# Gating the first eight raw weight loads of a fused attention and mixer kernel on the softmax broadcasts, in the plan that orders its instructions

## The chip, the cores and the metric

The kernel runs on one core of a Trainium2 chip. The metric is device time in microseconds (us) of one execution; of several runs the median counts. One further execution was taken with the hardware profiler; all rows below come from that one. PE is TensorE, with PEld for its weight loads; DVE is VectorE, ACT ScalarE, POOL GpSimd. SP, ACT and POOL issue the transfers between memories.

## The reference

Attention over 4 batches and 12 heads feeds a token mixer of rank 32 and a channel mixer. Cut to what matters:

```python
scores = cap * np.tanh((scale * q @ k.T) / cap)      # 448 x 448 a head, head_dim 64
attn = np.exp(scores - max); attn /= attn.sum(-1)
x = (attn @ v) laid out as [4, 448, 768]
h = x.transpose(0, 2, 1) @ U @ V                     # rank 32 over the tokens
u = x + h.transpose(0, 2, 1)
out = u + np.maximum(u @ w_ch1, 0.0) @ w_ch2         # 768 -> 3072 -> 768
```

## The kernel before

All work is written as tasks with estimated durations, buffers and priorities. `Plan.simulate` plays them through a list scheduler at build time: each engine takes the ready task of the lowest priority number. `emit` then writes the instructions in the order found. On the chip every engine and every issuing queue runs its own list in that order, and waits only where a semaphore for a real tile says so. A key in a task's `r` or `w` that is no tile (such as `("rd", p)`) orders tasks in the plan alone.

The first stage is attention, in groups of four of the 24 head pairs (`four`). A pair's scores are made on PE (`sc`, line 493), go through tanh (498) and exp (508) on ACT into `th`, are summed on DVE into `es` (540), and are multiplied with the values on PE (534) into `u`. For every second pair, p = 1, 3, ..., 23, `normalize(p)` runs what is called a chain here: sums over tokens on PE (573), a copy `sr`, a transfer `r<-sr` (580), a reciprocal on DVE (589), a transfer `rd<-r` to memory (584), and two transfers `rb<-rd` (597) that broadcast the rows over 64 partitions each. DVE multiplies `u` by `rb` (602, the norm), and only then can PE transpose `u` for the token mixer (`mixin`, 624). The three transfers are issued by POOL. There are 12 chains, the n-th for p = 2n - 1.

The second stage, the channel mixer, runs on PE from its first product (851) to the end, 12 steps of two row blocks of `w_ch1` and of `w_ch2` each, for two batches at a time. The weights come as 64-bit words. `block` loads a raw block of 768 KB into `wr` (SP queue, 720), ACT and DVE convert it into `wa` (`convert`: ACT 335, DVE 340 and 343, here called the join), ACT stores the result as `kept` (724), and DVE and ACT split it into parts (`ta` and `ws`, lines 691, 286 and 698). `wr` has two buffers, `wa` two during attention; blocks 1 to 4 serve the first step of the second stage, block 5 and on the next. One more `wr` buffer, between blocks 4 and 5, holds sums of `u`.

SP's queue issues `qk` (467) and `vn` (473), the inputs of attention, and the raw blocks, in one order. In what follows w1 to w5 are the loads of blocks 1 to 5.

Of the kernel before, what the change touches and what calls it, by code (L numbers as in the profile page):

```python
# [64 lines left out]
    ("operands", 56),  # L65
)
SLOW = {"four.load": 1.24, "normalize.spread": 1.00, "normalize.put": 1.25, "normalize.get": 0.72, "block.load": 1.02, "four.tanh": 1.99}
FILL, FIRST = 18, 5


# [220 lines left out]
class Build(Plan):  # L291
# [266 lines left out]
    def normalize(self, p):  # L558

        nc = self.nc  # L560
        prio = p - 100
        e = self.es[p - 1], self.es[p]
        rth, rj = self.rest[p]
        rest = p >= SUMS
        s = self.psum("misc")
        sr = self.buf("sr", [128, S], F32, self.an)
        r7 = self.buf("r7", [128, S // 32], F32, self.aq)
        u = self.u_bufs[p // NP]
        dram = {}

        def sums():
            for i in range(4):
                nc.tensor.matmul(
                    s.t[32 * i:32 * i + 32, :S], self.ones[:, 0], e[i % 2].t[:, i // 2], start=True, stop=not rest)
            for i in range(4 if rest else 0):
                nc.tensor.matmul(
                    s.t[32 * i:32 * i + 32, :S], self.ones[:, 1 + i % 2], rth.t[:, rj, i // 2], start=False, stop=True)

        def spread():
            nc.gpsimd.dma_start(out=r7.t, in_=sr.t[::32].rearrange("h (p f) -> h p f", p=32))  # L580

        def put():
            d = dram[0] = self.dp.tile([4, S], F32, tag="rd", name="rd", bufs=4)
            nc.gpsimd.dma_start(out=d.rearrange("a (p f) -> (a p) f", p=32), in_=r7.t)

        self.task({"PE": 1500 if rest else 750}, sums, r=[(e[0], 0), (e[1], 0), *([(rth, rj)] if rest else [])], w=[(s, 0)], prio=prio, mode="s")
        self.task({"DVE": 620, "ACT": 560}, lambda e: self.copy(e, sr.t, s.t[:, :S]), r=[(s, 0)], w=[(sr, 0)], prio=prio)
        self.task({"POOL": 700}, spread, r=[(sr, 0)], w=[(r7, 0)], lat=3000, prio=prio)
        self.task({"DVE": 250}, lambda: nc.vector.reciprocal(r7.t, r7.t), w=[(r7, 0)], prio=prio)
        self.task({"POOL": 600}, put, r=[(r7, 0)], w=[("rd", p)], lat=2500, prio=prio)  # L590
        rb = self.buf("rb", [128, 2, S], F32, self.an)
        q = p % NP - 1

        def get():
            rows = dram[0].rearrange("(a i) s -> a (i s)", a=2)
            for a in range(2):
                nc.gpsimd.dma_start(
                    out=rb.t[64 * a:64 * a + 64].rearrange("p i s -> p (i s)"), in_=rows[a:a + 1].broadcast_to((64, 2 * S)))

        def norm():  # L600
            x = u.t[:, q:q + 2]
            nc.vector.tensor_tensor(out=x, in0=x, in1=rb.t, op=ALU.mult)

        self.task({"POOL": 1100}, get, r=[("rd", p)], w=[(rb, 0)], lat=3400, prio=prio)
        self.task({"DVE": 1090}, norm, r=[(rb, 0)], w=[(u, q), (u, q + 1)], prio=prio, lock=True)

    def mixin(self, b, pp):
# [101 lines left out]
    def block(self, which, f, first, begin, prio):  # L709

        nc = self.nc
        a = self.buf("wa", [128, DM], F32, self.wp, self.late)
        if not first:
            self.task({"SP": 350}, lambda: nc.sync.dma_start(out=a.t, in_=self.kept[which, f]),
                r=[("kept", which, f)], w=[(a, 0)], lat=4000, prio=prio)
            return a
        raw = self.buf("wr", [128, 2 * DM], I32, self.wq)

        def load():
            nc.sync.dma_start(out=raw.t, in_=self.w[which][f].bitcast(I32))  # L720

        def keep():
            d = self.kept[which, f] = self.dp.tile([128, DM], F32, tag="kept", name="kept", bufs=2 * NF)
            nc.scalar.dma_start(out=d, in_=a.t)

        self.task({"SP": 350}, load, w=[(raw, "u"), (raw, "l")], lat=7500, prio=prio, begin=begin)
        self.convert(raw, lambda: raw.t, a, lambda: a.t, prio, DM)
        self.task({"ACT": 120}, keep, r=[(a, 0)], w=[("kept", which, f)], lat=6500, prio=prio)
        return a
# [37 lines left out]
    def moe(self):  # L767


        self.kept = {}  # L770
        order, pend = 10, None
        for n, bs in enumerate(((0, 1), (2, 3))):
            made = {}
            if not n:
                made[0] = self.prepare(0, True, 20000, ALONE - 90)
            xs = self.operands(bs, ORDER if n else EARLY, -50 if n else ALONE - 90)
            vs = self.buf("vs", [128, 3, S], F32, self.g1) if n else None
            gq, last, down, turns = {}, None, iter(()), [2] * 7
            for c in range(NCH):
                fs = [c * CF + i for i in range(CF)]  # L780
                ws, w1 = made.get(c) or self.prepare(c, n == 0, 0, 3 if n or c < NCH - 2 else -60)
                gs = {}
                if pend:
                    down, turns = self.down(order, *pend), [2] * 7
                    pend = None
                elif gq and c % 2 == 0:
                    down = self.down_seven(order, bs, c // 2 - 1, gq, vs)
                    gq = {}
                if n:
                    turns = [2] * 7 if not c else [1 + (i + c) % 2 for i in range(7)]  # L790
                if n and c == 0:
                    for _ in down:
                        pass
                    order += 12
                if n and c % 2 == 0:
                    pools = (self.g0, self.gw, self.g1) if c % 4 else (self.gw, self.g1, self.g0)
                    last = {(b, j): self.buf("gq", [128, 2, S], F32, *pools) for b, j in ((1, 1), (0, 0), (0, 1), (1, 0))}
                for k, _ in zip(turns, self.up_seven(bs, fs, xs, ws, gs, order, last if n else None, c % 2)):
                    for _ in range(k):
                        next(down, None)  # L800
                if not n or c % 2 or c == 0:
                    for _ in down:
                        pass
                if n:
                    if c % 2:
                        gq = last
                else:
                    pend = bs, fs, w1, gs
                order += 20
        self.last_sums(bs, vs)  # L810
        for _ in self.down_seven(order + 10, bs, PAIRS - 1, gq, vs):
            pass
# [209 lines left out]
    def down_seven(self, order, bs, m, gq, vs):  # L1022
# [4 lines left out]
        u0, u1 = (self.u_bufs[b] for b in bs)  # L1027
        block = lambda u, d: ((lambda: u.t[:, d]), (u, d))
        onto = {3: lambda d: block(u1, d), 1: lambda d: block(u0, d), 6: lambda d: block(u0, 3 + d), 5: lambda d: block(vs, d),
            2: lambda d: block(u0, d), 7: lambda d: block(u1, 3 + d), 4: lambda d: block(u0, 3 + d)}  # L1030
        if final:
            at = range(order, order + 21)
# [61 lines left out]
    def rank(self):  # L1094

        for t in self.tasks:
# [7 lines left out]
            if t.lat:  # L1104
                t.lat *= next((k for x, k in SLOW.items() if stage.startswith(x)), 1)

# [56 lines left out]
```

## Time and profile before

| | us |
|---|---|
| median of 3 runs | 853.18 |
| the runs | 852.47 to 858.34 |
| the profiled execution | 853.6 |
| its span, first to last instruction | 851.8 |
| busy in the span: PE / DVE / ACT / POOL | 840.4 / 691.0 / 527.6 / 146.1 |

The span is what the trace shows; the profiled execution is 1.8 us longer by the device's own clock, and 0.4 us above the median of the runs. Busy time of PE counts overlapping matmuls once, and a matmul's end is modelled.

### The profile page before, as it was taken

Reading aid. Unit: us, or ns where it says so; the run is one execution under the profiler, and the core shown is the slowest. Engines: PE = TensorE matmul, PEld = TensorE weight load, DVE = VectorE, ACT = ScalarE, POOL = GpSimd, SP = SyncE. Lnnn points to the kernel's source line nnn. Section 1 sums busy time; section 2 is a strip of 40 time slices with the busy share of each in tenths; the row PEclk is TensorE's granted clock in tenths of the full one; section 3 lists DMA queues with packets and bytes.
Section 4 is the critical chain, followed back from the end, with each engine's and each line's share of the span. In section 5 each row is a group of like instructions: output and inputs, shape, how many; then the busy total and the mean of one; then the engine's idle time right before and its main releaser. Section 6 shows DMA issues by size and latency. Waiting matters only on the chain. (4 is left out here: it accounts for less than half of the span.)

```text
span 851.8 us, 11737 instructions
## 1 busy us (share of the span) xinstructions
PE 840.4 (99%) x4264; PEld 671.4 (79%) x4264; DVE 691.0 (81%) x1144; ACT 527.6 (62%) x789; POOL 146.1 (17%) x188
## 2 busy tenths in 40 slices
PE   9999999998999999999999999999999999999998
PEld 5334334346899999999999899999999999999997
DVE  2799889999887777877778699789888788888786
ACT  7999899885555355545555465456655555656472
POOL 0111111111022122122122122102111111111142
PEclk9999999999999999999999999999999999999999
DMA  6752443423578878787877866714427354262479
GB/s 225 241 172 84 160 148 96 146 68 93 183 190 259 245 188 249 191 265 211 231 231 207 252 162 151 215 48 120 114 36 179 68 143 93 53 170 42 122 136 224
DMA packets 51354, 136.51 MB, mean 160 GB/s; under 512 B 6720, under 2 KB 27104, under 8 KB 51296
## 3 DMA queue, kind: packets, MB, share of 16 engines
q1 hardware_dynamic: 23024, 79.29, 28.3%
q0 software_dynamic: 21360, 37.59, 24.6%
q10 hardware_dynamic: 6912, 18.88, 5.7%
q8 instruction: 33, 0.54, 0.3%
q14 instruction: 25, 0.20, 0.1%
HBM read 79.28 MB, written 24.47 MB: 122 GB/s over the span
## 5 line engine op out<-in xcount | busy, mean ns | idle before, releaser
L851 PE MATMUL mm<-x,ws 128*128 128x448 f32 x1512 | 332.7, 367 | 1.4 <-ACT cx L284 0.8
L851 PEld LDWEIGHTS mm<-x,ws 128*128 128x128 f32 x1512 | 283.3, 188 | 27.3 <-ACT cx L284 1.2
L916 PE MATMUL mm<-g,w 128*128 128x448 f32 x864 | 187.0, 366 | 0.6 <-DVE cx L864 0.3
L916 PEld LDWEIGHTS mm<-g,w 128*128 128x128 f32 x864 | 162.0, 188 | 15.0 <-ACT st L284 0.9
L1049 PE MATMUL mm<-g,w 128*128 128x448 f32 x696 | 154.9, 366 | 0.0
L284 ACT ACTIVATE st<-mm 128x448 f32<-128x448 f32 x133 | 72.4, 544 | 113.7 <-PE mm L916 55.2
L1049 PEld LDWEIGHTS mm<-g,w 128*128 128x128 f32 x696 | 130.6, 188 | 11.8
L929 POOL DMA_DIRECT2D u<-st x72 | 62.5, 868 | 268.9 <-ACT st L284 263.8
L1084 POOL DMA_DIRECT2D u<-st x57 | 49.4, 866 | 224.1 <-ACT st L284 161.4
L498 ACT ACTIVATE th<-sc,qsc 128x896 f32<-128x896 f32 x84 | 80.3, 1005 | 11.9 <-PE sc L493 11.7
L493 PE MATMUL sc<-qk 64*128 64x448 f32 (+1 forms) x384 | 77.8, 573 | 0.0
L508 ACT ACTIVATE th<-th,capt 128x1792 f32<-128x1792 f32 x42 | 75.2, 1790 | 0.8
L921 DVE TENSOR_TENSOR u<-u,mm 128x448 f32<-128x448 f32 x72 | 44.5, 618 | 21.6 <-PE mm L916 19.9
L534 PE MATMUL o<-th,vn 128*64 128x448 f32 x288 | 59.4, 548 | 0.0
L493 PEld LDWEIGHTS sc<-qk 64*128 64x128 f32 (+1 forms) x384 | 27.2, 175 | 37.2 <-issue 18.9
L343 DVE SCALAR_TENSOR_TENSOR wa<-wa,wr 128x768 int32<-128x768 int32 (+2 forms) x50 | 46.7, 935 | 11.1 <-ACT wa L335 10.3
L698 DVE TENSOR_TENSOR ws<-ta,ws 128x384 fp32r<-128x384 f32 x96 | 53.0, 552 | 3.2 <-ACT ws L284 2.9
L1079 DVE TENSOR_TENSOR u<-u,mm 128x448 f32<-128x448 f32 x57 | 35.0, 619 | 23.3 <-PE mm L1049 21.7
L540 DVE TENSOR_TENSOR es<-es,th 128x896 f32<-128x896 f32 (+1 forms) x44 | 47.5, 1082 | 6.0 <-ACT th L508 5.5
L335 ACT ACTIVATE wa<-wr 128x768 f32<-128x768 f32 (+2 forms) x50 | 44.1, 884 | 3.8 <-DVE wr L340 2.4
L534 PEld LDWEIGHTS o<-th,vn 128*64 128x64 f32 x288 | 18.5, 136 | 32.8 <-issue 30.0
L284 ACT ACTIVATE ws<-ta 128x384 fp32r<-128x384 f32 x64 | 32.9, 519 | 15.2 <-PE mm L851 8.9
(118 smaller groups left out, 957.5 us busy)
## 6 DMA issues: line engine op xcount, KB each, us to landing
wr<-in_w SPq DMA_DIRECT2D x48, 768.0 KB, 5.7
u<-st POOLq DMA_DIRECT2D x129, 224.0 KB, 4.1
kept<-wa ACTq DMA_DIRECT2D x48, 384.0 KB, 5.8
qk<-in_qk SPq DMA_DIRECT2D x24, 448.0 KB, 4.0
wr<-kept SPq DMA_DIRECT2D x24, 384.0 KB, 3.7
wa<-kept SPq DMA_DIRECT2D x24, 384.0 KB, 4.0
vn<-in_v SPq DMA_DIRECT2D x12, 448.0 KB, 3.7
rb<-rd POOLq DMA_DIRECT2D x24, 224.0 KB, 3.7
```

The costliest lines, as they stand in the source:

```text
L284: e.activation(out=out, in_=in_, func=func)
L493: nc.tensor.matmul(ps.t[out, a, :S], qks[c].t[hd, 1, 128 * t:min(S, 128 * t + 128)], qks[c].t[hd, 0], start=True, stop=True)
L498: nc.scalar.activation(out=th.t[:, j], in_=ps.t[:, :, :S], func=AF.Tanh, scale=self.qsc)
L508: nc.scalar.activation(out=th.t, in_=th.t, func=AF.Exp, scale=self.capt)
L534: nc.tensor.matmul(o.t[64 * a:64 * a + 64, :S], vn.t[:, 3 * i + t, a], th.t[:, j, a], start=False, stop=t == 2)
L540: e.tensor_tensor(out=out(), in0=in0(), in1=in1(), op=ALU.add)
L698: e.tensor_tensor(out=lo, in0=src(), in1=hi.bitcast(F32), op=ALU.subtract)
L851: nc.tensor.matmul(ps.t[:, :S], ws[p].t[:, wi, sl], xs[p].t[:, xi, d], start=fresh and n == 0, stop=n == 8, skip_group_check=not fresh)
L916: nc.tensor.matmul(ps.t[:, :S], w1[f].t[:, wi, sl], g[b, f].t[:, gi], start=f == fs[0] and i == 0, stop=f == fs[-1] and i == 2)
L929: nc.gpsimd.dma_start(out=u.t[:, d], in_=st.t, accum_op=ALU.add)
L1049: nc.tensor.matmul(ps.t[:, :S], w[:, wi, k, sl], g[gi][:, k], start=fresh and n == 0, stop=n == 5, skip_group_check=not fresh)
L1084: self.task({"POOL": 1000}, lambda: nc.gpsimd.dma_start(out=out(), in_=st.t, accum_op=ALU.add), r=[(st, 0)], w=[key], lat=6000, prio=-200)
```

## The change

A table AFTER names, for the n-th raw block, the chain p = 2n - 1. The load task of that block gets the key `("got", p)` among what it reads, and the task that issues the chain's two broadcasts gets it among what it writes. So in the plan the n-th load is not ready before the n-th chain's broadcast is estimated to have landed. Blocks beyond the eighth have no such key. The key names no tile.

```diff
+AFTER = (1, 3, 5, 7, 9, 11, 13, 15)
...
-        self.task({"POOL": 1100}, get, r=[("rd", p)], w=[(rb, 0)], lat=3400, prio=prio)
+        self.task({"POOL": 1100}, get, r=[("rd", p)], w=[(rb, 0), ("got", p)], lat=3400, prio=prio)
...
+        n = self.blocks = self.blocks + 1
+        after = [("got", p) for p in AFTER[n - 1:n]]
...
-        self.task({"SP": 350}, load, w=[(raw, "u"), (raw, "l")], lat=7500, prio=prio, begin=begin)
+        self.task({"SP": 350}, load, r=after, w=[(raw, "u"), (raw, "l")], lat=7500, prio=prio, begin=begin)
...
-        self.kept = {}
+        self.kept, self.blocks = {}, 0
```

First place: SP's queue from the seventh `qk` load on, before, with the semaphores that each instruction waits for (DMAHW: an earlier transfer of SP or ACT; PE, DVE, Activation: that engine). The rows `wr<-in_w` are w1 to w4.

```order
L467 DMA qk<-in_qk 128x896 [waits DMAHW4_49,PE_49]
L720 DMA wr<-in_w 128x1536 [waits DMAHW5_49,DMAHW2_49,DVE_49]
L720 DMA wr<-in_w 128x1536 [waits DMAHW6_49,DMAHW3_49,DVE_49]
L473 DMA vn<-in_v 128x896 [waits DMAHW7_49,PE_49]
L467 DMA qk<-in_qk 128x896 [waits DMAHW0_49,PE_49]
L467 DMA qk<-in_qk 128x896 [waits DMAHW1_49,PE_49]
L720 DMA wr<-in_w 128x1536 [waits DMAHW5_49,DVE_49]
L473 DMA vn<-in_v 128x896 [waits DMAHW4_49,PE_49]
L467 DMA qk<-in_qk 128x896 [waits PE_49]
L467 DMA qk<-in_qk 128x896 [waits DMAHW6_49,PE_49]
L720 DMA wr<-in_w 128x1536 [waits DMAHW7_49,DVE_49]
```

The same queue in the changed kernel, from the tenth `qk` load on; w1 to w4 again.

```order
L468 DMA qk<-in_qk 128x896 [waits DMAHW1_49,PE_49]
L723 DMA wr<-in_w 128x1536 [waits DMAHW2_49,DVE_49]
L468 DMA qk<-in_qk 128x896 [waits DMAHW3_49,PE_49]
L723 DMA wr<-in_w 128x1536 [waits DMAHW4_49,DVE_49]
L474 DMA vn<-in_v 128x896 [waits DMAHW5_49,PE_49]
L468 DMA qk<-in_qk 128x896 [waits DMAHW6_49,PE_49]
L468 DMA qk<-in_qk 128x896 [waits DMAHW0_49,PE_49]
L474 DMA vn<-in_v 128x896 [waits DMAHW2_49,PE_49]
L723 DMA wr<-in_w 128x1536 [waits DMAHW3_49,DVE_49,Activation_49]
L474 DMA vn<-in_v 128x896 [waits DMAHW5_49,DMAHW4_49,PE_49]
L723 DMA wr<-in_w 128x1536 [waits DVE_49]
```

w1 and w2 moved from behind the seventh `qk` load to behind the tenth and eleventh, w3 and w4 from behind the ninth and eleventh to around the seventh `vn`; w5 moved from behind the seventeenth `qk` load to behind the eighteenth. No load waits for a transfer of POOL.

Second place: DVE's list up to the second norm (line 602, the row on `rb`), before. `es` are the sums of attention, `wa`, `ta` and `ws` the converted and split weights, `xx` and `ys` the token mixer.

```order
L540 TENSOR_TENSOR es<-th 128x896
L691 TENSOR_TENSOR ta<-wa 128x384 x2
L635 TENSOR_TENSOR xx<-misc,xx 112x512
L286 CAST ws<-ta 128x384
L286 CAST ws<-wa 128x384
L698 TENSOR_TENSOR ws<-ta,ws 128x384
L540 TENSOR_TENSOR es<-es,th 128x896
L286 CAST ys<-misc 128x256
L540 TENSOR_TENSOR es<-es,th 64x896
L651 TENSOR_TENSOR ys<-misc,ys 32x256
L286 COPY u_197<-o_387 128x448
L602 TENSOR_TENSOR u_197<-u_197,rb 128x896
```

The same stretch in the changed kernel, up to its second norm (line 603).

```order
L541 TENSOR_TENSOR es<-th 128x896
L341 TENSOR_SCALAR wr<-wr 128x768
L636 TENSOR_TENSOR xx<-misc,xx 112x512
L541 TENSOR_TENSOR es<-es,th 128x896
L287 CAST ys<-misc 128x256
L541 TENSOR_TENSOR es<-es,th 64x896
L652 TENSOR_TENSOR ys<-misc,ys 32x256
L287 COPY u_197<-o_375 128x448
L603 TENSOR_TENSOR u_197<-u_197,rb 128x896
```

The splitting of the first block moved behind the second norm, and so did, further up in the list, two joins (line 343) and two of the three shifts of raw words (line 340).

## Rows read from the trace of the kernel before

**Rows 1.** The page, part 1: busy us, share of the span, instructions.

```profile
PE 840.4 (99%) x4264; PEld 671.4 (79%) x4264; DVE 691.0 (81%) x1144; ACT 527.6 (62%) x789; POOL 146.1 (17%) x188
```

**Rows 2.** Stretches: length, busy PE, PEld, DVE, ACT, POOL; clock; DMA share, GB/s.

```profile
0.00:847.70 847.70, 840.44 (x4264) 671.40 (x4264) 690.37 (x1143) 527.55 (x789) 146.13 (x188) 1.00 0.59 160
...
57.00:194.00 137.00, 136.03 (x787) 54.93 (x787) 124.47 (x181) 126.59 (x127) 20.73 (x36) 1.00 0.39 119
194.00:220.00 26.00, 23.21 (x129) 17.69 (x126) 24.70 (x46) 13.79 (x29) 2.82 (x5) 1.00 0.36 112
```

**Rows 3.** PE and DVE timelines near two norms; in brackets idle time and its ender.

```profile
43.61 0.65 PE L624 MATMUL misc<-ident,u 128*112 128x128 f32 x4 [1.69 <-DVE u L602]
...
39.49 1.09 DVE L540 TENSOR_TENSOR es<-th 128x896 f32<-128x896 f32 x1
42.46 1.09 DVE L602 TENSOR_TENSOR u<-u,rb 128x896 f32<-128x896 f32 x1 [1.88 <-DMA rb<-rd]
...
56.77 1.09 DVE L602 TENSOR_TENSOR u<-u,rb 128x896 f32<-128x896 f32 x1 [0.38 <-DMA rb<-rd]
```

**Rows 4.** POOL's timeline: the first chain's broadcasts and the seventh's first transfer.

```profile
35.04 1.06 POOL L597 DMA_DIRECT2D rb<-rd  x2 [1.46 <-DMA rd<-r]
...
124.38 0.73 POOL L580 DMA_DIRECT2D r<-sr  x1 [11.41 <-DVE sr L286]
```

**Rows 5.** SP's queue: start, length, what was issued (two at once: first to last).

```profile
21.22 3.35 SPq L720 DMA_DIRECT2D wr<-in_w  x2
...
33.99 0.33 SPq L720 DMA_DIRECT2D wr<-in_w  x1
...
39.17 9.73 SPq L467 DMA_DIRECT2D qk<-in_qk  x2
49.14 0.33 SPq L720 DMA_DIRECT2D wr<-in_w  x1
...
69.40 18.02 SPq L473 DMA_DIRECT2D vn<-in_v  x2
...
113.41 0.37 SPq L720 DMA_DIRECT2D wr<-in_w  x1
...
120.23 5.16 SPq L467 DMA_DIRECT2D qk<-in_qk  x2
```

**Rows 6.** Transfers issued in 33:43, 49:58, 66:73, 130:137, 179:187: last number, us to landing.

```profile
rb<-rd POOLq DMA_DIRECT2D x2, 224.0 KB, 6.5
...
r<-sr POOLq DMA_DIRECT2D x1, 7.0 KB, 3.1
...
wr<-in_w SPq DMA_DIRECT2D x1, 768.0 KB, 6.2
rb<-rd POOLq DMA_DIRECT2D x2, 224.0 KB, 6.1
...
rb<-rd POOLq DMA_DIRECT2D x2, 224.0 KB, 3.6
...
rb<-rd POOLq DMA_DIRECT2D x2, 224.0 KB, 5.2
...
r<-sr POOLq DMA_DIRECT2D x1, 7.0 KB, 2.3
```

**Rows 7.** Groups by line and form: busy us, mean ns of one, idle before.

```profile
L340 DVE TENSOR_SCALAR wr<-wr 128x768 int32<-128x768 int32 x48 | 26.6, 556 | 2.1 <-DMA wr<-in_w 2.0
L343 DVE SCALAR_TENSOR_TENSOR wa<-wa,wr 128x768 int32<-128x768 int32 x48 | 45.7, 955 | 9.3 <-ACT wa L335 8.4
L691 DVE TENSOR_TENSOR ta<-wa 128x384 f32<-128x384 f32 x48 | 25.4, 552 | 5.1 <-DMA wa<-kept 5.0
L286 DVE CAST ws<-ta 128x384 fp32r<-128x384 f32 x32 | 11.4, 357 | 8.5 <-PE mm L851 7.8
L698 DVE TENSOR_TENSOR ws<-ta,ws 128x384 fp32r<-128x384 f32 x96 | 53.0, 552 | 3.2 <-ACT ws L284 2.9
```

**Rows 8.** PE's timeline: the first product of the second stage.

```profile
196.69 2.09 PE L851 MATMUL mm<-x,ws 128*128 128x448 f32 x9
```

## Prediction

> **What bounds the kernel now.** I read the busy times first. PE is busy for 840.4 of 851.8 us [rows 1], and the matmul ends are modelled, so the share alone proves little. The stretches say more: up to the end of PE's last matmul at 847.70 its busy time is 840.44, so 7.26 us is all the time that PE stood still in the whole kernel [rows 2]. In attention from 57 to 194 it is idle for 137 - 136.03 = 0.97 us, although ACT is busy for 126.59 and DVE for 124.47 of the same 137. The three engines are close to each other there. At the handover to the second stage, 194 to 220, PE is idle for 26 - 23.21 = 2.79 us while DVE is busy for 24.70 of 26. With the 1.69 us named below, 7.26 - 0.97 - 2.79 - 1.69 = 1.8 us are left for all the rest. So the work of PE is fixed, and a new order of the others can win only those 7.26 us, or add to them.
>
> Then I looked for gaps that a raw weight load can have caused. There is one large one. PE waits 1.69 us at 43.61 for the first norm; DVE waited 1.88 us for the broadcast `rb` of the first chain [rows 3]. POOL issued that broadcast at 35.04 [rows 4], and it took 6.5 us to land, where the third chain's took 3.6 [rows 6]. In flight beside it were w3, issued at 33.99, one store `kept`, one `vn` and one `qk` load [rows 5]. The second chain's broadcast is as slow, 6.1 us, beside w4 (issued at 49.14), but DVE waited only 0.38 us for it, at 56.77, and PE not at all [rows 3, 5, 6]. w1 and w2 come before the first chain's transfers, and w5 at 113.41 is the last load in attention that can collide.
>
> **What the change does on the chip.** The key is no tile, and the order shows that w1 to w5 wait for PE's, ACT's or DVE's semaphores and for earlier loads, never for POOL's transfers. So nothing holds a load until a broadcast lands. What changes is the place of the loads in SP's queue, and with it the planned order on ACT, DVE and PE.
>
> From SP's order and the times before: w1 comes behind the tenth `qk` load, at about 39.2; w2 behind the eleventh, at about 48.9 (the pair of `qk` loads runs from 39.17 to 39.17 + 9.73); w3 and w4 stand around the two `vn` loads, at about 69.7 and 87.4; w5 behind a `qk` load of 120.23, at about 120.6 [rows 5]. The buffers are free by then: w3 and w4 need the joins of blocks 1 and 2, which stand right behind the second norm and ahead of the fourth chain's reciprocal in DVE's list.
>
> **Term 1, the first chain.** w3 and the `kept` store leave the time of its broadcast; `vn` and `qk` stay. The trace has no broadcast with exactly these neighbours. The nearest row is the seventh chain's, with a `vn` and a `qk` load beside it: 5.2 us [rows 6]. The ends are 3.6 us (the third chain's) and 6.5 us (as now, if w1 at 39.2 hurts as w3 did). DVE was free at 39.49 + 1.09 = 40.58 [rows 3]; with 5.2 us the broadcast lands at about 35.04 + 0.53 + 5.2 = 40.8 (0.53 is half of the 1.06 that the two issues take, rows 4). That leaves 0.2 us of DVE's wait, and PE's gap of 1.69 goes nearly whole. I take -1.7; the bounds are 0 and -1.7.
>
> **Term 2, new collisions.** The second chain keeps its neighbour (w2 at 48.9 where w4 was at 49.14): 0. w3 at 69.7 can meet the tail of the third chain's broadcast, which was issued after 66 and took 3.6 us [rows 6]; w4 at 87.4 falls between two chains: 0. w5 at 120.6 now covers the start of the seventh chain, whose `r<-sr` starts at 124.38, since a raw block takes 5 to 6.2 us to land [rows 4, 6]. Beside a load `r<-sr` took 3.1 us, alone 2.3 [rows 6], so that chain comes 0.8 us later. Bounds: 0 (another wait ends last) and 2.9 (all that separates a crowded broadcast from a free one, 6.5 - 3.6). I take +0.8.
>
> **Term 3, DVE's work moved back.** Ahead of the second norm DVE loses two shifts, two joins, two `ta`, two casts and one `ws`: 2 x 0.556 + 2 x 0.955 + 2 x 0.552 + 2 x 0.357 + 0.552 = 5.4 us [rows 7]. They come behind it instead, where DVE already works for 124.47 of 137 us [rows 2]. Its idle time there is 12.5 us, more than twice what arrives, so the cover is the waiting that DVE does for ACT and PE. If that cover holds, the cost is 0; if none of it can be used (each wait sits behind an in-order instruction), the norms and sums come up to 5.4 us later, and PE, which has only 0.97 us of gap there, shifts with them. I take 0, by the larger idle time. ACT loses two conversions early and gets them back later, under the same cover. The `kept` stores move with them, to a time when fewer loads are in flight.
>
> **Term 4, the handover.** PE's 2.79 us of gaps at 194 to 220 depend on which DVE and ACT rows stand ahead of the first results, and these rows are reshuffled. They can vanish or double: -2.8 to +2.8, taken as 0, since the same work stands on both sides.
>
> The sum against the profiled execution is 853.6 - 1.7 + 0.8 = 852.7. That execution is 0.4 us above the median, so against 853.18 the forecast is **852.3 us**.
>
> **Rivals.**
>
> The load does as much harm at its new place. Nothing holds w1 until the first broadcast has landed: at 39.2 it enters while the first one is still on its way (35.04 + 0.53 + 3.6 = 39.2 at the earliest, 42.1 if it stays at 6.5). Then term 1 is 0 and term 2 stays: 853.2 to 854.0. For it speaks that the order has no such wait; against it that most of the broadcast has moved by then.
>
> Slower: DVE's crowding, the other end of term 3. Its place is behind the second norm, from 57 to 194. It decides as soon as DVE's idle time there cannot be filled by the moved work; with half to all of the 5.4 us lost and terms 1 and 2 kept, the time is 855.0 to 857.7, centre 856. For it speaks that ACT, DVE and PE are all above 90% busy there, so that a late sum has no slack to be caught up in; against it DVE's 12.5 us.
>
> Larger gain: the new order also closes the other gaps. All 7.26 us of PE's idle time gone would be 845.9, and not even that is 1% faster. Term 1 and half of the rest, (7.26 - 1.7) / 2 = 2.8, would be 853.18 - 1.7 - 2.8 = 848.7.
>
> Late weights. The first product that needs a split weight runs at 196.69 [rows 8]; w2 would land at about 48.9 + 6.2 = 55 and w4 at about 94, so about 100 us are left for conversions that take DVE 0.556 + 0.955 us each [rows 7]. If that cover failed, PE would stall by whatever the split is late, and only a lateness of 8.5 us or more would show as above 1%. The Trainium skill (DMA: Bandwidth & Descriptors, Rules for kernel authors) says to issue a DMA early and to wait on its semaphore late, and by that rule alone holding back a load is a loss. The rows above leave it no room here: early enough is already reached with some 100 us to spare.
>
> **How the numbers follow.** A measurement of this kernel tells about 1% from no change: 8.5 us, so faster means below 844.6 and slower above 861.7. Chances: the forecast 0.60 (its own range with term 4 is 849.5 to 855.1), crowding of DVE 0.22, equal harm 0.13, the larger gain 0.03, late weights or another stall of many us 0.02. The range from 849.5 to 857.7 holds the forecast, equal harm and the crowding, and leaves out the last two and what noise of single runs does to a median (one of the three runs was 858.34). No case reaches 1% faster, so 0.01 there; above 1% slower I leave 0.04, the late weights and a crowding worse than all of term 3.
>
> **What the changed kernel's profile would show.** Term 1: the first chain's broadcast lands in about 4 to 5 us, and PE's gap of 1.69 us ahead of the first transposes is gone. Term 2: w5 at 120 to 121 and a seventh chain whose `r<-sr` takes about 3 us. Term 3: from 57 to 194 DVE is busy for about 5 us more and PE idle for no more than about 1 us; rising gaps of PE that end on DVE there would show the crowding. Term 4: PE's idle time between the last score and 220. The first product stands within 2 us of 195. The forecast is wrong if PE's idle time up to its last matmul is above 9 or below 4 us, or if PE's busy time itself changes, which none of these steps would explain.

## The result, and the profile after

| | before | changed |
|---|---|---|
| median of 16 runs | 853.67 us | 862.21 us |
| the runs | 852.47 to 860.57 | 857.14 to 867.16 |
| profiled execution, its span | 853.6, 851.8 | 862.97, 861.2 |

The ratio is 1.0081, 95% interval 1.0056 to 1.0106: the change costs 8.5 us by the medians and 0.81%, 6.9 us, by the ratio, where I had forecast a gain of 0.9. Of the two profiled executions the changed one is 9.4 us longer.

The page, part 1, and the stretches that answer to [rows 1, 2], of the changed kernel:

```profile
PE 845.4 (98%) x4264; PEld 674.4 (78%) x4264; DVE 693.6 (81%) x1149; ACT 526.2 (61%) x784; POOL 146.2 (17%) x188
```

```profile
0.00:857.10 857.10, 845.45 (x4264) 674.37 (x4264) 692.98 (x1148) 526.21 (x784) 146.19 (x188) 0.99 0.58 158
...
194.00:220.00 26.00, 21.92 (x110) 15.28 (x107) 21.61 (x39) 13.74 (x25) 4.47 (x8) 0.87 0.36 109
...
58.00:60.00 2.00, 0.99 (x9) 0.26 (x10) 2.00 (x4) 0.48 (x1) 0.00 (x0) 1.00 0.02 7
60.00:62.00 2.00, 2.00 (x10) 1.03 (x12) 2.00 (x4) 0.60 (x1) 0.70 (x1) 0.67 0.40 157
62.00:64.00 2.00, 2.00 (x8) 0.59 (x6) 1.95 (x3) 1.31 (x2) 0.04 (x1) 0.50 0.24 48
...
212.00:214.00 2.00, 1.80 (x7) 1.42 (x7) 2.00 (x4) 1.82 (x4) 0.30 (x2) 0.50 0.02 4
214.00:216.00 2.00, 2.00 (x7) 1.78 (x6) 1.60 (x4) 0.00 (x0) 1.05 (x2) 0.50 0.34 97
```

Up to its last matmul PE stands still for 857.10 - 845.45 = 11.65 us, 4.4 more than before. But its busy time has grown too, by 845.45 - 840.44 = 5.0 us for the same 4264 matmuls. The reason stands in the third number from the right, the granted clock: it was 1.00 all through the profiled execution of the kernel before, and is 0.50 (1.2 of 2.4 GHz) in two places here, at 61 to 64 and at 211 to 217. So half of the 9.4 us is PE standing still, and half is PE working slowly.

PE's timeline there, with the idle time and its ender in brackets:

```profile
59.01 0.96 PE L574 MATMUL misc<-es,ones 128*32 128x448 f32 x8 [2.59 <-DVE u L665]
...
60.48 3.18 PE L494 MATMUL sc<-qk 64*128 64x448 f32 x8
...
199.02 2.07 PE L854 MATMUL mm<-x,ws 128*128 128x448 f32 x9
...
205.37 0.96 PE L574 MATMUL misc<-es,ones 128*32 128x448 f32 x8 [1.09 <-DVE u L665]
...
208.67 0.47 PE L641 MATMUL misc<-xx,ust 112*128 112x256 f32 x2 [1.01 <-DVE xx L287]
...
213.13 3.56 PE L854 MATMUL mm<-x,ws 128*128 128x448 f32 x9
```

The gap of 1.69 us of [rows 3] is gone. In its place stands one of 2.59 us ahead of the third chain's sums, and the scores behind it take 3.18 us instead of 1.77. At the handover the gaps of 1.09 and 1.01 us are new (before had none above 0.81 there), and the product behind them takes 3.56 us, where the stage's first product takes 2.07 (2.09 in [rows 8]).

Where the first gap comes from is read on DVE, POOL and SP, and in the transfers issued from 38 to 42 and from 46 to 50 (last number: us to landing):

```profile
38.94 1.09 DVE L603 TENSOR_TENSOR u<-u,rb 128x896 f32<-128x896 f32 x1 [0.22 <-DMA rb<-rd]
46.13 0.24 DVE L590 RECIPROCAL r<-r 128x14 f32<-128x14 f32 x1 [0.82 <-DMA r<-sr]
56.33 1.09 DVE L603 TENSOR_TENSOR u<-u,rb 128x896 f32<-128x896 f32 x1 [2.08 <-DMA rb<-rd]
```

```profile
40.62 0.72 POOL L581 DMA_DIRECT2D r<-sr  x1 [4.87 <-ACT sr L285]
46.67 0.58 POOL L585 DMA_DIRECT2D rd<-r  x1 [5.33 <-DVE r L590]
52.03 1.05 POOL L598 DMA_DIRECT2D rb<-rd  x2 [4.78 <-DMA rd<-r]
```

```profile
39.23 0.38 SPq L723 DMA_DIRECT2D wr<-in_w  x1
46.43 0.33 SPq L468 DMA_DIRECT2D qk<-in_qk  x1
46.85 0.38 SPq L723 DMA_DIRECT2D wr<-in_w  x1
```

```profile
wr<-in_w SPq DMA_DIRECT2D x1, 768.0 KB, 6.7
...
r<-sr POOLq DMA_DIRECT2D x1, 7.0 KB, 5.5
```

```profile
wr<-in_w SPq DMA_DIRECT2D x1, 768.0 KB, 5.3
...
rd<-r POOLq DMA_DIRECT2D x1, 7.0 KB, 4.8
```

The first norm is on time (a wait of 0.22 us, where it was 1.88). The second chain is the one that is hit, twice: w1 goes 1.4 us ahead of its `r<-sr`, and w2 within 0.2 us of its `rd<-r`. Both transfers move 7 KB and land about when the raw load beside them does: `r<-sr` at 40.62 + 5.5 = 46.1 and w1 at 39.23 + 6.7 = 45.9, `rd<-r` at 51.5 and w2 at 52.1. The second norm then waits 2.08 us for the broadcast.

### The profile page after: what moved, and what is told of

The parts are those of the page before. It is cut to its first block, busy times and chain, and to the rows that moved or that the text cites. A ratio compares the mean times of both kernels' runs of the same rounds, so it can differ in the third digit from the quotient of the medians.

```text
span 861.2 us, 11736 instructions
## 1 busy us (share of the span) xinstructions
PE 845.4 (98%) x4264; PEld 674.4 (78%) x4264; DVE 693.6 (81%) x1149; ACT 526.2 (61%) x784; POOL 146.2 (17%) x188
```

## The experiments

The median of before is 853.67 to 856.14 us from one set of runs to the next, so each kernel is judged by its ratio to before on the same chip. Most kernels change only the order that is written out. `plans` plays the scheduler twice, with the new keys and without; `placed(first, second, cut)` writes the first order up to a cut and what is then left in the second's order; `moved` moves single rows and leaves the order of all others.

| kernel | median | ratio to before, 95% |
|---|---|---|
| changed | 862.21 | 1.0081 (1.0056 to 1.0106) |
| w2_late | 857.72 | 1.0023 (1.0008 to 1.0038) |
| w1_early | 859.00 | 1.0049 (1.0027 to 1.0071) |
| all_early | 856.72 | 1.0010 (0.9996 to 1.0023) |
| early_then_before | 854.80 | 0.9986 (0.9972 to 0.9999) |
| late_turn | 857.40 | 1.0015 (1.0002 to 1.0028) |
| second_part | 859.29 | 1.0048 (1.0030 to 1.0065) |
| first_part | 864.88 | 1.0119 (1.0080 to 1.0159) |
| first_early | 862.96 | 1.0086 (1.0064 to 1.0108) |
| filled | 860.14 | 1.0060 (1.0037 to 1.0082) |
| filled_twice | 860.17 | 1.0067 (1.0041 to 1.0093) |
| all_early_filled | 855.66 | 1.0000 (0.9984 to 1.0015) |
| best_filled | 853.69 | 0.9992 (0.9977 to 1.0007) |

### The place of w1 and w2

**w2_late**: one load one place later.

```diff
+        n = next(n for n, r in enumerate(rows) if r[0] is loads[1])
+        row = rows.pop(n)
+        k = [m for m, r in enumerate(rows) if m >= n and r[1] == "SP"][0]
+        rows.insert(k + 1, row)
```

> The changed kernel with one instruction moved: w2's load stands one place later in SP's queue, behind the vn load of 53.2 instead of ahead of it; every other engine keeps the changed order. Theory (w2 delays the second chain's `rd` write, and PE's gap behind it costs twice, once as a gap and once in the clock): `rd` takes 1.5 to 1.7 us, the broadcast is issued near 48.7, PE's gap of 2.59 us at 59 and the half clock behind it are gone; PE is 4 us earlier from there on, and the time is 858 (862.2 - 4.3). Rival 1, crowding of DVE by the conversions moved back: w2's place does not matter, 861 to 863. Rival 2, w2 now meets the tail of the broadcast: `rd` is quick but `rb` takes 6 us, the gap shrinks to under 1 us, 859.5 to 861.

The ratio fell by 0.0058, 5.0 us, where the theory had 4.3. `rd<-r` took 1.7 us and the clock stayed full. But the gap stayed as well, at 1.34 us, and for a reason that the theory had not named: `r<-sr`, beside w1, took 7.7 us, because w1 itself took 8.9. Two lines of the transfers from 38 to 58:

```profile
r<-sr POOLq DMA_DIRECT2D x1, 7.0 KB, 7.7
rd<-r POOLq DMA_DIRECT2D x1, 7.0 KB, 1.7
```

**w1_early**: the other load alone, moved behind the seventh `qk` load (and behind the last use of its buffer).

```diff
+        for w in (0,):
+            n = next(n for n, r in enumerate(rows) if r[0] is loads[w])
+            row = rows.pop(n)
+            k = [m for m, r in enumerate(rows) if any(b.tag == "qk" for b in r[0].bufs) and r[1] == "SP"][6]
+            k = max(k, *(m for m, r in enumerate(rows) if any(b.tag == "wr" and b.i == w for b in r[0].bufs)))
+            rows.insert(k + 1, row)
```

> The changed kernel with w1 alone loaded where the kernel before loads it, behind the seventh qk load; w2 stays behind the eleventh qk load, near 46.9. Theory (each small transfer of the second chain suffers from the raw load that is in flight beside it): `r<-sr` takes 2.5 us without w1, `rd<-r` is issued at about 45.6, a good 1 us ahead of w2, and takes 2 us, `rb` beside w2 takes 6 us as before; PE's gap ahead of the third sums is 1 to 1.5 us, and the ratio to before is 1.002, as in w2_late. Rival, w2 alone does the harm: `rd` still takes 4 us or more, the gap is over 2 us, the ratio 1.006 or more.

The profile does what the theory said: `r<-sr` 2.8 us, `rd<-r` issued at 46.05 and landed in 1.7, `rb` 6.2, PE's gap 1.22. The ratio, 1.0049, lies between the two forecasts, so it confirms neither. The profiled execution, 857.75 us, is one of the quicker of ten: three took 861.5 to 863.1 us at a mean granted clock of 0.992 or 0.993, against its 0.996, and no profile shows where they lost it.

```profile
rb<-rd POOLq DMA_DIRECT2D x2, 224.0 KB, 6.2
...
r<-sr POOLq DMA_DIRECT2D x1, 7.0 KB, 2.8
rd<-r POOLq DMA_DIRECT2D x1, 7.0 KB, 1.7
```

**all_early**: both (`for w in (0, 1)`), every other instruction where the change puts it.

> The changed kernel, its order kept on PE, ACT, DVE and POOL, with w1 and w2 loaded where the kernel before loads them, behind the seventh qk load. Theory (the raw loads beside the second chain's two small transfers cost the first part): `r<-sr` takes about 2.5 us and `rd<-r` 1.8, as in first_early, PE's gap ahead of the third sums is about 0.5 us at full clock, and PE is 3.8 us earlier than in the changed kernel from there on: 858.4, with the handover's gaps and half clock as they are. Rival 1, the late conversions cost time by themselves: 860 or more. Rival 2, the handover eats what was won: 861 to 862.

856.72 us, 1.0010: the loss of 0.81% is down to 0.10%, more than expected. The transfers, the second norm (no wait) and PE's third sums:

```profile
r<-sr POOLq DMA_DIRECT2D x1, 7.0 KB, 2.7
rd<-r POOLq DMA_DIRECT2D x1, 7.0 KB, 1.8
```

```profile
54.16 1.09 DVE L603 TENSOR_TENSOR u<-u,rb 128x896 f32<-128x896 f32 x1
```

```profile
56.84 0.96 PE L574 MATMUL misc<-es,ones 128*32 128x448 f32 x8 [0.54 <-DVE u L665]
58.31 1.77 PE L494 MATMUL sc<-qk 64*128 64x448 f32 x8
```

The conversions, the `kept` stores and the order of ACT, DVE and PE are still the changed ones. So it is the two loads' place in SP's queue that costs (1.0081 - 1.0010) x 855 = 6.1 us, and not the later conversions. PE loses less than the two transfers do: in all_early DVE takes up `r<-sr` 1.9 us and the broadcast 1.6 us after they have landed, and that slack takes in part of the delay.

### Why 6 us, when one profile shows 4

By the third mix (PE's third pair of matmuls at line 661, which starts at 74.28 against 70.47 in all_early) the profiled execution of the changed kernel had lost 3.8 us. To see whether it was a typical one, I took four more of the same kernel.

> The changed kernel once more, for another profiled execution. Theory (the second chain's transfers take another time in each execution, and that is what spreads the changed kernel's runs from 857 to 867): the second norm stands between 55 and 59.5, and the four executions again1 to again4 come in the order of their second norms, about 1 us or more of time for each us of norm: 858 to 860 for a norm near 55.3, 864 or more for one near 59. Rival, the spread comes from the handover or the second stage: the norms agree within 0.5 us, or their order is not that of the times.

> As again1: the order of the four times follows the order of the second norms, or, by the rival, it does not.

> As again1: the order of the four times follows the order of the second norms, or, by the rival, it does not.

> As again1: the order of the four times follows the order of the second norms, or, by the rival, it does not.

| execution | us | `r<-sr` | `rd<-r` | second norm | PE's gap ahead of the third sums | third mix |
|---|---|---|---|---|---|---|
| changed, as above | 862.97 | 5.5 | 4.8 | 56.33 | 2.59 | 74.28 |
| again1 | 868.04 | 6.4 | 4.8 | 60.10 | 6.02 | 79.14 |
| again2 | 862.91 | 6.6 | 4.5 | 59.79 | 6.30 | 77.56 |
| again3 | 864.75 | 6.9 | 3.9 | 57.92 | 4.62 | 77.14 |
| again4 | 861.70 | 6.0 | 4.8 | 57.93 | 4.85 | 76.57 |

The first profile was the mildest of five. The other four reach the third mix 6.1 to 8.7 us behind all_early, which agrees with the 6.1 us of the ratios. A milder one yet is that of first_part (below), which has the changed order up to about 119 us: its w1 took 5.4 us, `r<-sr` 4.3 and `rd<-r`, a good 1 us ahead of w2, 2.1, and it reached the third mix at 72.14. The mean granted clock of the sixteen runs says the same without a trace: the four with 0.996 or more took 857.1 to 859.4 us, the twelve with less took 859.2 to 867.2. In all_early, with the half clock at the handover alone, the profiled execution has 0.996. Without the two raw loads the second norm hardly varies: 53.91 to 54.18 in the five kernels that load w1 and w2 early. The order of the times is not that of the norms, though: again2 has the second latest norm and the second best time. Its half clock at the handover was the shorter by half (2-us stretches of 0.97, 0.50 and 0.68, against 0.91, 0.50, 0.50, 0.50 and 0.88 in again3). So the second chain's transfers are part of the spread, not all of it. Its broadcast varies too: 3.5, 5.3, 5.6, 4.2 and 4.5 us in the order of the table. again1, PE and the clock:

```profile
62.78 1.72 PE L574 MATMUL misc<-es,ones 128*32 128x448 f32 x8 [6.02 <-DVE u L665]
```

```profile
62.00:64.00 2.00, 1.22 (x8) 0.20 (x8) 2.00 (x4) 0.00 (x0) 0.00 (x0) 0.50 0.00 0
64.00:66.00 2.00, 2.00 (x10) 1.19 (x8) 1.56 (x3) 0.43 (x1) 0.39 (x1) 0.50 0.49 194
66.00:68.00 2.00, 2.00 (x8) 0.68 (x4) 1.99 (x4) 0.79 (x2) 0.34 (x1) 0.50 0.14 12
```

### The order behind it

**first_part** and **second_part** cut the two orders at the sixth chain's broadcast.

```diff
+        order = self.placed(gated, plain, lambda rows: [t for t, _ in rows].index(self.writer[("got", 11)]))
...
+        order = self.placed(plain, gated, lambda rows: [t for t, _ in rows].index(self.writer[("got", 11)]))
```

> The changed order on all engines up to the issue of the sixth chain's broadcast, the order of before from there to the end. At that point the two plans have done the same conversions. Theory (two separate places): only the second chain's loss stays, 2.2 us by the sixth mix (135.41 to 137.64): 855.7, and the handover at 194 to 220 has PE gaps under 3 us at full clock. Rival, crowding of DVE: all moved work is done in this part, so the whole loss must come with it: 860 to 862.

> The converse: the order of before up to the issue of the sixth chain's broadcast, the changed order from there to the end. Theory (two separate places): the handover's loss alone, 9.4 - 2.2 = 7.2 us: 860.7, with a granted clock below 0.9 at 200 to 220. Rival 1, crowding in the first part: 853 to 854. Rival 2, the handover only breaks because PE arrives there late: 853 to 855.

first_part fits neither theory: 864.88. Its own seam, where the one order passes into the other, stalls, with gaps at 119 to 128 and a clock of 0.83 at 120 to 140 that neither parent has, so its time tells nothing of the handover:

```profile
119.64 0.65 PE L661 MATMUL misc<-vst,ys 128*128 128x448 f32 x2 [1.06 <-DVE ys L652]
125.06 1.50 PE L574 MATMUL misc<-es,ones 128*32 128x448 f32 x2 [2.15 <-DVE u L665]
```

second_part is 3.8 us above before, not the 7.2 of the theory. It shows something else: up to there it has the order of before, yet in its profiled execution, the slowest of its twelve, PE's gap ahead of the first transposes was 2.03 us instead of 1.69, and the clock fell behind it (0.62 and 0.52 from 44 to 48). So the gap of [rows 3] can probably cost a half clock in the kernel before as well: in the 35 executions of before that were run with all_early the mean clock goes from 1.00 down to 0.995. No profile of before shows where.

```profile
43.84 0.65 PE L625 MATMUL misc<-ident,u 128*112 128x128 f32 x4 [2.03 <-DVE u L603]
...
46.11 3.34 PE L535 MATMUL o<-th,vn 128*64 128x448 f32 x12
```

**first_early** is first_part with the two loads moved as in all_early.

> first_part with w1 and w2 loaded where the kernel before loads them (two loads behind the seventh qk load); w3 and w4 stay at 70 and 87, and the conversions stay where the change put them. Theory: both the first and the second chain then run without a raw load beside them, PE is 2.15 us ahead of before from 55 on as the changed kernel was at that point, and with the handover of before the time is 851.3 (853.5 - 2.15). Rival 1, crowding: the conversions behind the second norm still cost, 853.5 to 856. Rival 2, the handover eats an earlier arrival, because the products wait for something else there: 853 to 854.

The same seam stalls again (4.1 us of gaps at 117 to 126), and hides in the 862.96 us what the rest gained. Up to 60 us it does what was expected: `r<-sr` 2.5, `rd<-r` 1.8, second norm at 54.18.

**early_then_before** and **late_turn** cut where the two orders differ by a single finished task, near 165 us. early_then_before also has all_early's move.

```diff
+        order = self.placed(gated, plain, lambda rows: 605)
...
+        order = self.placed(plain, gated, lambda rows: 605)
```

> all_early up to the tenth chain's sums, near 165 us, and the order of before from there to the end. At that point the two plans differ by a single task done, so that the seam should not stall as the one of first_part did. Theory (the handover's loss is its order): the first part is about 2 us ahead of before, the handover costs what it costs before: 852.5 if before is at 854.5, the fastest of all kernels so far. Rival 1, the handover's gaps come with any other arrival: 856 to 859. Rival 2, the seam stalls: gaps of over 1 us of PE at 160 to 180.

> The converse of early_then_before: the order of before up to the tenth chain's sums, near 165 us, the changed order from there. The raw loads all stand as before. Theory: the handover's order alone costs 4 to 5 us, of which over 1 us in more gaps and 2 us or more at the half clock: 858.5 to 859.5 if before is at 854.5. Rival, the handover's loss comes from the earlier part of the order: 854 to 855.

early_then_before is 1.3 us under before, where 2 were expected, and the only kernel whose interval ends below 1, if barely. It stalls nowhere at its seam. Against all_early, which differs from it only behind 165 us, it wins 856.72 - 854.80 = 1.9 us. late_turn costs 0.15%, 1.3 us, less than the 4 to 5 expected, though its profile has the changed handover's gaps (4.27 us at 190 to 230, before 2.75) and a clock of 0.91 at 200 to 220. The handover's new order costs 1 to 2 us.

### The clock

**filled** keeps PE busy in the gap ahead of the third sums.

```diff
+            for n in range(12):
+                i, a = n // 2 % 2, n % 2
+                rows = slice(64 * i, 64 * i + 64)
+                self.nc.tensor.matmul(os[i].t[64 * a:64 * a + 64, :S], vn.t[rows, 6, a], rth.t[rows, rj, a], start=True, stop=True)
+            fn()
```

> The changed kernel with twelve matmuls more on PE, copies of those of line 523 ahead of the third sums, where PE waits 2.59 us; their results are written over, so that they only keep PE busy, for 2.6 us. Theory (the half clock behind the gap is caused by PE standing still): the granted clock is full at 60 to 66, the scores behind the gap take 1.77 us instead of 3.18 and the av matmuls 2.48, and the time is 1.65 us lower, 860.5. Rival 1, the clock falls for another reason: the scores still take 3 us, 862 to 863. Rival 2, the clock is back but ACT and DVE set the pace there: scores of 1.77 us, and no gain, 862.

In its profile the scores took 1.77 us at full clock, and the median is 860.14. Neither proves the theory. Its chain was a quick one (second norm at 55.32), and the ratios 1.0060 and 1.0081 overlap in their intervals.

**all_early_filled**, **filled_twice** and **best_filled** fill the handover's gaps (best_filled only the one, with five matmuls).

```diff
+                    self.nc.tensor.matmul(mm.t[:, :S], x.t[:, 0, 0, :128], x.t[:, 0, 0], start=True, stop=True)
```

> all_early with fourteen matmuls more on PE in its gaps at the handover (five after the mix of 199.8, five and four after the transposes of 203.1 and 206.1), into the bank of the next product, whose first matmul writes over them. They take 2.9 us of 3.0 us of gaps. Theory (PE standing still lowers the clock, and the lower clock is most of what the handover's new order costs): the product behind the gaps takes 2.1 us instead of 3.56, the granted clock is 0.95 or more at 200 to 220, and the time is 1.5 to 2.5 us under all_early's, a ratio of 0.998 to 0.9995 to before. Rival 1, the gaps and not the clock are the cost: the product takes 2.1 us and the ratio stays at 1.001. Rival 2, the clock falls in spite of the filling: 3 us or more for the product.

> The changed kernel with both fillings, that of filled at the second chain and that of all_early_filled at the handover; all loads stay where the change puts them. Theory: both half clocks are gone; the handover's gives back 2 us on top of filled's ratio of 1.006, so 1.0035 to 1.004; what is left above before are gaps of PE. Rival, the clock is not the cost: the ratio stays at 1.006 to 1.008.

> early_then_before with five matmuls more on PE in the handover's gap of 1.09 us at 204.3, into the bank of the next product. Theory: the product behind it takes 2.1 us instead of 3.3, and the time is 1.2 us under early_then_before's, a ratio of 0.997, the fastest of all. Rival, its typical run has no half clock there in the first place (some of its runs show a mean clock of 1.0): the ratio stays at 0.9986.

At the handover the clock follows PE's standing still. In all 11 profiled executions with the changed order there and no filling it fell to half; in the two with that order and the filling, all_early_filled and filled_twice, it did not. All 12 executions of all_early_filled have a mean clock of 0.999 or 1.000, all 12 of all_early one of 0.995 to 0.998. The order of before is not free of it: in early_then_before the clock fell as well, behind gaps of 0.26, 1.09 and 0.28 us, and in best_filled, with the middle one filled, it stayed full. But it stayed full in first_part as well, behind gaps of 0.20, 0.28, 1.08 and 0.30 us, so which row of gaps costs the clock is not settled.

```profile
205.34 0.51 PE L641 MATMUL misc<-xx,ust 112*128 112x256 f32 x2 [1.09 <-ACT xx L285]
...
206.70 3.32 PE L854 MATMUL mm<-x,ws 128*128 128x448 f32 x9
```

The same product, in all_early and then in all_early_filled, and a stretch beside each:

```profile
209.18 3.56 PE L854 MATMUL mm<-x,ws 128*128 128x448 f32 x9
```

```profile
208.00:210.00 2.00, 1.81 (x7) 1.43 (x7) 2.00 (x4) 1.88 (x4) 0.34 (x1) 0.50 0.02 4
```

```profile
209.36 2.02 PE L854 MATMUL mm<-x,ws 128*128 128x448 f32 x9
```

```profile
208.00:210.00 2.00, 1.49 (x8) 1.24 (x9) 2.00 (x5) 2.00 (x5) 0.57 (x1) 1.00 0.02 4
```

What this is worth stays open: all_early_filled is 0.0010 under all_early and best_filled 0.0006 above early_then_before, both within the intervals, where I had expected 1.5 to 2.5 and 1.2 us. In filled_twice, 1.0067 instead of 1.0035, the second chain's filling was too short: this execution had its second norm at 59.07, PE stood still for 3.34 us in spite of 2.49 us of filling, and the clock fell to 0.61 and 0.54.

```profile
61.75 1.10 PE L574 MATMUL misc<-es,ones 128*32 128x448 f32 x8 [3.34 <-DVE u L665]
```

## Why the prediction was wrong

**Term 1 was right.** The first chain's broadcast is free of w3 and of the `kept` store (no run tells the two apart) and took 3.5 us, just under the lower end of 3.6. DVE waits 0.22 us, and PE's gap is gone. With the two loads early and the handover of before, the kernel keeps 1.2 us of it (0.9986 of 855), barely clear of noise.

**Term 2 failed**, in its first sentence: "The second chain keeps its neighbour (w2 at 48.9 where w4 was at 49.14): 0." It measured about 6 us, and three things were wrong in it. First, the time: I left the eleventh `qk` load where it stands before, at 48.6 to 48.9 [rows 5]. That load waits for PE, which term 1 had just made earlier, so it went at 46.43 and w2 at 46.85, on top of `rd<-r`. Secondly, in the second chain I looked at the broadcast alone and passed over the two small transfers; w1 at 39.2 has the chain's `r<-sr` right behind it. Thirdly, the price: my row for a small transfer beside a load gave 3.1 us against 2.3 [rows 6], and the five executions of the changed kernel show 5.5 to 6.9 for `r<-sr` and 3.9 to 4.8 for `rd<-r`. That row had no raw load beside it. Before, w3 went at 33.99 and landed 5.2 us later, at 39.2, and `r<-sr` was issued 2.4 us after that; the loads in flight beside it were the `vn` of 37.32 and the `qk` of 39.17. Both lines, of the transfers issued from 33 to 36 and of POOL's timeline before:

```profile
wr<-in_w SPq DMA_DIRECT2D x1, 768.0 KB, 5.2
```

```profile
41.58 0.71 POOL L580 DMA_DIRECT2D r<-sr  x1 [5.47 <-ACT sr L284]
```

The two delays add up, since the chain is serial. The Trainium skill (DMA: Bandwidth & Descriptors, Issuing engines are not separate DMA queues) says that transfers started by different engines run on the same 16 engines and interleave. The runs agree that they share: with w1 in flight the transfer on POOL's queue took 5.5 us, in all_early 2.7. Of an interleaving of the two they show nothing, since the small transfer lands behind the load (last section).

**The w5 part of term 2**, +0.8, did not come. w5 was issued at 122.15 and took 7.0 us in the changed kernel's trace, so it was in flight when the seventh chain's `r<-sr` went at 126.90, but that took 2.5 us, as it did before (2.5); in the four further executions it took 2.5 to 2.9. w5's row, and of the transfers issued from 126 to 128 the small one:

```profile
122.15 0.38 SPq L723 DMA_DIRECT2D wr<-in_w  x1
```

```profile
r<-sr POOLq DMA_DIRECT2D x1, 7.0 KB, 2.5
```

What w3 and w4 do at their new places was not singled out by any run.

**Term 3 held.** DVE's moved work was not the cost: all_early keeps all of it and is at 1.0010. In early_then_before PE is idle for 137 - 135.14 = 1.86 us from 57 to 194, 0.9 more than in [rows 2]; that is the most that can be laid to it. Its sign came out weaker than forecast: from 57 to 194 DVE was busy 1.5 us more in early_then_before and 2.6 more in all_early, not 5.

**Term 4 was mis-sized**: taken as 0 within 2.8, measured 1.3 (late_turn) to 1.9 us (all_early against early_then_before).

**A term was missing**: PE's own speed. I wrote that the work of PE is fixed and that nothing in my steps would explain another busy time. In the profiled pair it grew by 5.0 us, at 61 to 64 and 211 to 217 by the halved clock.

The sum by what was measured: -1.2 for term 1 and what goes with it, +1.9 for the handover, +6.1 for the second chain, together 6.8 us, 0.8%. That it closes proves nothing new, since each term is the difference of two neighbouring kernels. Of the rivals "equal harm at its new place" came nearest: the loads do more harm there. But it had priced the first chain only, and that one was not hit: its broadcast, issued at 34.68, had landed before w1 went at 39.23.

## What to carry to other kernels

A load that is moved lands beside other transfers: list all that are in flight in its new place, the small ones of a serial chain above all, and compute its issue anew from what its queue waits for, because the change itself moves that. A row prices such a meeting only if its two transfers were in flight at the same time. An idle gap of PE can cost twice, once as a gap and once in the clock behind it. Where a cost is contention, one profile is one draw: take several before a number of it is trusted.

## What the runs showed of the hardware

The second chain's `r<-sr`, 7 KB, took 2.3 to 3.3 us in the nine executions with no raw load in flight beside it and 4.2 to 7.7 in the nine with w1 issued 1.4 us ahead of it. What decided was how long the load took: w1's own time was 5.4 to 8.9 us there, and in all nine `r<-sr` landed 0.2 to 0.3 us behind w1. `rd<-r`, as small, did the same: in five executions it was issued 0.2 to 1.3 us behind w2, took 3.9 to 5.1 us and landed about 0.2 us behind w2; in first_part, filled and w1_early it was issued 1.1 us ahead of w2 and took 1.7 to 2.1. In the changed kernel's first trace, 0.2 us ahead was too little: 4.8 us. Why w1 took so different times stays open. In five executions of one kernel the second norm stood anywhere from 56.33 to 60.10.

The granted clock went to half behind single gaps of PE of 2.03, 2.59, 3.34 and 4.62 to 6.30 us, and stayed full behind 1.69 [rows 3], 1.34 and 1.22 us. Length alone does not decide it: in first_part it also stayed full behind 2.39 us, at the same place as the 2.59.

```profile
58.51 0.96 PE L574 MATMUL misc<-es,ones 128*32 128x448 f32 x8 [2.39 <-DVE u L665]
...
59.98 1.77 PE L494 MATMUL sc<-qk 64*128 64x448 f32 x8
```

It also fell behind the handover's row of gaps of 1.09, 1.01, 0.57 and 0.89 us, none of which is that long, and in the changed kernel it was still 1.00 at 58 to 60, while PE stood still, and fell when PE had resumed. The Trainium skill (TensorE: Matmul & The Clock Gate, Part 1) says that the point at which the clock rises differs from run to run. The runs agree, for both directions: behind nearly the same gaps at the handover the clock fell 2.7 us ahead of the product in again3 and 0.7 us ahead of it in again2, and the half clock lasted twice as long in again3.
